# Local and strided attention with a gated MLP on one core: a constant tile of 636 bytes made 1024 bytes wide

## The chip, the core and the metric

The kernel runs on one core of a Trainium2 chip. A core has a matrix engine (TensorE, PE in the profile, with its weight loads listed apart as PEld), a vector engine (VectorE, DVE), a scalar engine (ScalarE, ACT), GpSimd (POOL) and SyncE (SP), which here issues the transfers. They share an on-chip memory of 128 partitions (SBUF) and the accumulators that TensorE writes (PSUM). The metric is the device time of one execution in microseconds, as the median of several runs. Addresses below are byte offsets inside a partition; they are the same in all 128 partitions.

## The reference

`q`, `k` and `v` have shape (8, 8, 576, 64): batch, heads, sequence, head dimension. The first four heads use a local mask of 32 positions, the other four a strided one; the result goes through a gated MLP whose gate is `erf(softplus(h))`.

```python
scores = scale * np.matmul(q, k.transpose(0, 1, 3, 2))
mask_local = (rel >= 0) & (rel < stride)                       # stride = 32
mask_strided = (rel >= 0) & (pos[None, :] % stride == pos[:, None] % stride)
masks = np.stack([mask_local if h < H // 2 else mask_strided for h in range(H)], axis=0)
scores = np.where(masks[None, :, :, :], scores, -1000000000.0)
scores = scores - np.max(scores, axis=-1, keepdims=True)
attn = np.exp(scores)
attn = attn / (np.sum(attn, axis=-1, keepdims=True) + 1e-09)
x = np.matmul(attn, v)                 # then (4608, 512)
h = x @ w_in                           # w_in 512 x 2048
sp = np.maximum(h, 0.0) + np.log1p(np.exp(-np.abs(h)))
out = (h * erf(sp)) @ w_out            # w_out 2048 x 512
```

## The kernel before

**The work.** The 4608 tokens are cut into 12 chunks of 384. For each chunk and each of 16 blocks of 128 hidden columns, `mm1` (L725) makes twelve matmuls: the weights are blocks of 128 columns of `pair` tiles (`w_in` split in a high and a low part), and the moving operand is a slice of 384 columns of `xhi` or `xlo`, the attention output in the same split. Four ACT tanh steps (L733) and DVE steps between them (L730, L754) form the gate; L757 and L760 split the product into `ghi` and `glo`. `mm2` (L788) then makes nine matmuls (three for each 128 tokens) with slices of `ghi` and `glo` as weights and 512 columns of a `pair` tile (`w_out`) as the moving operand. `mm1` runs 2304 matmuls in all, `mm2` 1728.

**Attention.** Batches 0 and 1 go through `piece`: scores (L302), the first mask added by TensorE (L312), a maximum over the partitions on POOL (L328), its subtraction (by TensorE with the tile `neg` for batch 0, by DVE for batch 1), exponential on ACT, product with `v` (L345). The other batches go through `quad`: scores (L502, in 64x64 tiles of the array, or L490), the second mask applied by a DVE minimum with the tile `cap` (L520), maximum and sum on POOL (L528, L548), product with `v` (L592). L617 and L622 write the result into `xhi` and `xlo`.

**The weights.** They arrive as 64-bit words in `words` tiles and are turned into 32-bit floats by DVE (L677, L684, L690), then split by ACT (L695) and DVE (L698) into `pair` tiles, which take the place of the `words` tiles in the same memory.

**What sets the order.** A planner (`Plan`) gives each operation an assumed duration and a key, works out one order for each engine and emits the instructions in it. Tiles' addresses do not enter it. SyncE issues all transfers from one queue in the planner's order.

**Where the tiles lie.** Pools give out addresses in the order in which tiles are first made, each rounded up to 32 bytes. In the built program the eight `xhi` and `xlo` tiles begin at 16512 and follow each other at 4608 bytes; `ident` is at 53376, `con` (first mask) at 53888, `cap` (second mask) at 54784. `cap` has 2·96 + 126 = 318 bf16 elements, 636 bytes, and so takes 640. Behind it stand `neg` at 55424, then two `qk` buffers (55936 and 58976), three `v` buffers (62016, 63072, 64128), the `sm`, `mx`, `tt` and `r` buffers of the attention, three `ob`, two `a`, two `ghi` and two `glo` buffers (79648 to 95007), and from 95008 on the 32 weight tiles `words`/`pair` of 4096 bytes each. The last one ends at 226080.

The lines that make the constants:

```python
con = cpool.tile([P, NCON], BF16, name="con")
cap = cpool.tile([P, 2 * QL + QS], BF16, name="cap")
cap_l = cap[:, : 2 * QL].rearrange("p (b h q) -> p b h q", b=2, h=1)
cap_s = cap[:, 2 * QL :].rearrange("p (u q) -> p u q", u=1)
neg = cpool.tile([P, P], F32, name="neg")
```

Of the kernel before, what the change touches and what calls it, by code (L numbers as in the profile page):

```python
# [10 lines left out]
BF16 = mybir.dt.bfloat16  # L11
# [7 lines left out]
P = 128  # L19
# [6 lines left out]
SW = 512  # L26
# [23 lines left out]
QL = 96  # L50
RB = 7
NA = S // 32
QS = RB * NA
# [143 lines left out]
def attention_moe(  # L197
# [13 lines left out]
    cpool = ctx.enter_context(tc.tile_pool(name="cpool", bufs=1))  # L211
# [11 lines left out]
    mask_l = con[:, : 2 * QL].rearrange("p (b h q) -> p b h q", b=2, h=1)  # L223
    mask_s = con[:, 2 * QL : 2 * QL + QS].rearrange("p (u q) -> p u q", u=1)
    ident_b = con[:, 2 * QL + QS :]
    cap = cpool.tile([P, 2 * QL + QS], BF16, name="cap")
    cap_l = cap[:, : 2 * QL].rearrange("p (b h q) -> p b h q", b=2, h=1)
    cap_s = cap[:, 2 * QL :].rearrange("p (u q) -> p u q", u=1)
    neg = cpool.tile([P, P], F32, name="neg")
# [792 lines left out]
```

## Time and profile before

| | us |
|---|---|
| median of 3 runs | 945.45 |
| the runs | 944.45 to 946.5 |
| the profiled execution's own time | 944.03 |
| its span, first to last instruction | 942.3 |
| TensorE busy in the span | 930.5 |
| DVE busy | 679.0 |
| ACT busy | 576.6 |
| POOL busy | 324.5 |

The span is what the profile covers; the profiled execution's own time is 1.73 us longer. "Busy" counts the time in which an engine had at least one instruction running, so an engine can be busy without working at its peak. The lists by line give a group's busy time, the mean duration of one instruction and the idle time ahead of it; the chain of waits follows the work back from the last instruction.

### The profile page before, as it was taken

The page shows a single profiled execution, that of the slowest core. Times are in us where ns is not written, and L with a number is a line of the kernel's source. Part 1 is how long each engine was busy: PE and PEld are TensorE (multiplying, and loading weights), DVE is VectorE, ACT ScalarE, POOL GpSimd, SP SyncE. Part 2 cuts the span into 40 slices and gives each one's busy share as a digit, 9 for nine tenths or more (in the row PEclk, how much of TensorE's full clock was granted, in tenths as well). Part 3 has the DMA queues.
Part 4 walks back from the last instruction along what each step waited for, and adds up shares of the span by engine and source line. Part 5 has one row for each costly group of instructions (what it writes and reads, how often), then busy time and mean ns, then how long its engine had stood idle before and what let it go on. Part 6 is the DMA issues. An engine that isn't in the chain of part 4 may idle for free.

```text
span 942.3 us, 16156 instructions
## 1 busy us (share of the span) xinstructions
PE 930.5 (99%) x5993; PEld 820.0 (87%) x5993; DVE 679.0 (72%) x1539; ACT 576.6 (61%) x1283; POOL 324.5 (34%) x160
## 2 busy tenths in 40 slices
PE   8999999999999999999999999999999999999998
PEld 6788898888888888888888888888888888999997
DVE  5999998667777777666867777775777776455553
ACT  4776677556566656556556655665655656555654
POOL 4443104525263444513535643342535353000000
PEclk9999999999999999999999999999999999999999
DMA  8987202111212113102112111211211210000000
GB/s 285 303 316 253 65 16 79 39 45 58 77 50 79 48 47 105 39 12 81 54 54 93 51 47 51 79 38 34 90 47 49 81 46 4 34 1 0 34 1 34
DMA packets 37663, 68.83 MB, mean 73 GB/s; under 512 B 4176, under 2 KB 18640, under 8 KB 37584
## 3 DMA queue, kind: packets, MB, share of 16 engines
q1 hardware_dynamic: 37584, 67.80, 22.0%
q8 instruction: 47, 0.77, 0.3%
q14 instruction: 32, 0.26, 0.1%
HBM read 58.34 MB, written 9.44 MB: 72 GB/s over the span
## 4 chain that ended last, share of the span: by engine, by line
PE 92%; DVE 5%; DMA 2%; ACT 0%; issue 0%; SPq 0%
PE o L788 42%; PE h L725 41%; PE ps L592 3%; PE ps L502 2%; DVE w L684 1%; DVE w L690 1%; PE s L302 1%; DVE w L677 1%; DVE a L730 1%; DVE pair L698 1%; DMA qk<-qk_str 1%; DMA words<-w_in 1%; PE ps L490 0%; DVE xlo L399 0%; PE ps L302 0%; PE av L345 0%
## 5 line engine op out<-in xcount | busy, mean ns | idle before, releaser
L788 PE MATMUL o<-pair,ghi 128*128 128x512 f32 x1152 | 366.3, 399 | 0.0
L733 ACT ACTIVATE a<-a 128x384 f32<-128x384 f32 x576 | 292.0, 522 | 94.4 <-DVE a L730 86.4
L730 DVE SCALAR_TENSOR_TENSOR a<-a,h 128x384 f32<-128x384 f32 x384 | 210.9, 550 | 170.7 <-ACT a L733 167.8
L725 PE MATMUL h<-xhi,pair 128*128 128x384 f32 x1536 | 303.7, 339 | 1.5 <-DVE glo L760 1.4
L725 PEld LDWEIGHTS h<-xhi,pair 128*128 128x128 f32 x1536 | 273.9, 188 | 10.5 <-DVE glo L760 2.3
L788 PEld LDWEIGHTS o<-pair,ghi 128*128 128x128 f32 x1152 | 209.5, 188 | 43.8 <-issue 1.5
L788 PE MATMUL o<-pair,glo 128*128 128x512 f32 x576 | 224.9, 390 | 0.0
L528 POOL PARTITION_ALL_REDUCE mx<-sm x66 | 100.0, 1558 | 357.3 <-DVE sm L520 348.4
L548 POOL PARTITION_ALL_REDUCE su<-sm x66 | 182.0, 2801 | 43.2 <-ACT sm L542 43.2
L733 ACT ACTIVATE a<-h 128x384 f32<-128x384 f32 x192 | 94.2, 491 | 148.7 <-PE h L725 148.2
L725 PE MATMUL h<-xlo,pair 128*128 128x384 f32 x768 | 166.3, 338 | 0.0
L725 PEld LDWEIGHTS h<-xlo,pair 128*128 128x128 f32 x768 | 138.1, 188 | 0.0
L754 DVE TENSOR_TENSOR h<-a,h 128x384 f32<-128x384 f32 x192 | 106.9, 557 | 42.2 <-ACT a L733 42.1
L788 PEld LDWEIGHTS o<-pair,glo 128*128 128x128 f32 x576 | 108.2, 188 | 24.2
L757 ACT CAST ghi<-h 128x384 fp32r<-128x384 f32 x192 | 91.3, 476 | 59.0 <-PE o L788 57.7
L760 DVE TENSOR_TENSOR glo<-h,ghi 128x384 fp32r<-128x384 f32 x192 | 105.4, 549 | 20.2 <-ACT ghi L757 16.7
L328 POOL PARTITION_ALL_REDUCE mx<-sm x24 | 42.4, 1776 | 63.0 <-ACT sm L320 55.5
L542 ACT ACTIVATE sm<-sm 128x384 f32<-128x384 f32 (+2 forms) x66 | 36.2, 553 | 18.6 <-DVE sm L535 17.8
L535 DVE TENSOR_TENSOR sm<-sm,mx 128x384 f32<-128x384 f32 (+2 forms) x66 | 39.9, 614 | 0.2
L520 DVE TENSOR_TENSOR sm<-ps,cap 128x384 f32<-128x384 f32 (+2 forms) x66 | 37.0, 586 | 0.0
L592 PEld LDWEIGHTS ps<-sm,v 128*64 128x64 f32 x528 | 24.6, 136 | 9.2 <-issue 6.7
L592 PE MATMUL ps<-sm,v 128*64 128x96 f32 (+2 forms) x528 | 31.7, 260 | 0.0
(59 smaller groups left out, 532.6 us busy)
## 6 DMA issues: line engine op xcount, KB each, us to landing
qk<-qk_loc SPq DMA_DIRECT2D x48, 304.0 KB, 3.2
qk<-qk_str SPq DMA_DIRECT2D x32, 380.0 KB, 3.7
v<-v_all SPq DMA_DIRECT2D x80, 130.0 KB, 2.2
out<-ob SPq DMA_DIRECT2D x36, 256.0 KB, 2.1
words<-w_in SPq DMA_DIRECT2D x16, 512.0 KB, 5.1
words<-w_out SPq DMA_DIRECT2D x16, 512.0 KB, 4.6
qk<-qk_str SPq DMA_DIRECT2D x16, 136.0 KB, 2.6
v<-v_all SPq DMA_DIRECT2D x16, 65.0 KB, 1.9
```

What stands on the lines that cost most here:

```text
L328: yield nc.gpsimd.partition_all_reduce(mx[:, :cols], sm[:, :cols], P, ReduceOp.max)
L528: yield nc.gpsimd.partition_all_reduce(mx[k][:, :cols], sm[k][:, :cols], P, ReduceOp.max)
L535: yield nc.vector.tensor_tensor(out=d, in0=d, in1=mx[k][:, :cols], op=ALU.subtract)
L548: yield nc.gpsimd.partition_all_reduce(su[k][:, :cols], sm[k][:, :cols], P, ReduceOp.add)
L592: yield nc.tensor.matmul(px[h * D : (h + 1) * D, c0 : c0 + n], v[i][:, blk, h, :D], sm[bank][:, c : c + n], start=True, stop=True,)
L725: yield nc.tensor.matmul(ph[:, :CH], win[4 * s + cc][:, w, fs], x[cc][:, c0 : c0 + CH], start=(i == 0), stop=(i == len(terms) - 1))
L730: yield nc.vector.scalar_tensor_tensor(out=out, in0=in0, scalar=scalar, in1=in1, op0=op0, op1=op1)
L733: yield nc.scalar.activation(dst, src, func, bias=bias[i], scale=scale)
L754: yield nc.vector.tensor_tensor(out=ph[:, :CH], in0=a.tile, in1=ph[:, :CH], op=ALU.mult)
L757: yield nc.scalar.copy(ghi.tile, ph[:, :CH])
L760: yield nc.vector.tensor_tensor(out=glo.tile, in0=ph[:, :CH], in1=ghi.tile.bitcast(F32), op=ALU.subtract)
L788: yield nc.tensor.matmul(po.tile, g[:, ts], wout[f][:, w], start=(f == 0 and i == 0), stop=(f == NFC - 1 and i == 2),)
```

## The change

`cap` is made with 512 bf16 columns (1024 bytes) instead of 318, and the name `cap` then stands for its first 318 columns. Everything that writes or reads `cap` sees the same 318 columns at the same address, 54784. Every tile behind it begins 384 bytes higher: `neg` at 55808 instead of 55424, the first weight tile at 95392 instead of 95008, and so on to the last, which ends at 226464. `xhi`, `xlo`, `ident`, `con` and `cap` stay where they were. The built programs hold the same instructions in the same order, with the same waits, on all five engines.

384 is three times 128, so every moved address keeps its remainder by 128 and changes it by 256 and by 512. The weight tiles go from 288 to 160 in remainders by 512.

```diff
-    cap = cpool.tile([P, 2 * QL + QS], BF16, name="cap")
+    cap = cpool.tile([P, SW], BF16, name="cap")[:, : 2 * QL + QS]
```

`SW` is 512, `QL` 96 and `QS` 126.

## The prediction, on record before the change was run

> **What bounds the kernel now.** I read the page's totals first.
>
> ```profile
> span 942.3 us, 16156 instructions
> ...
> PE 930.5 (99%) x5993; PEld 820.0 (87%) x5993; DVE 679.0 (72%) x1539; ACT 576.6 (61%) x1283; POOL 324.5 (34%) x160
> ...
> PEclk9999999999999999999999999999999999999999
> ...
> PE 92%; DVE 5%; DMA 2%; ACT 0%; issue 0%; SPq 0%
> ```
>
> TensorE has something running in 99% of the span, its granted clock is full in every slice, and 92% of the chain that ended last is TensorE's. The remaining 7% are DVE and transfers. The view of busy time by stretches (PE, PEld, DVE, ACT, POOL) tells where they lie:
>
> ```profile
> 0.00:33.00 33.00, 27.84 (x176) 20.78 (x177) 22.19 (x52) 18.61 (x52) 15.68 (x13) 1.00 0.87 280
> 33.00:74.00 41.00, 38.78 (x260) 33.14 (x258) 40.63 (x96) 30.54 (x82) 15.55 (x8) 1.00 0.92 327
> 74.00:116.00 42.00, 41.38 (x275) 35.63 (x274) 41.84 (x103) 26.57 (x62) 11.39 (x7) 1.00 0.44 140
> 116.00:790.00 674.00, 674.00 (x4549) 596.39 (x4549) 499.02 (x1147) 413.39 (x904) 281.83 (x132) 1.00 0.18 56
> 790.00:942.30 152.30, 148.53 (x742) 134.08 (x738) 75.31 (x146) 87.48 (x185) 0.00 (x0) 1.00 0.04 16
> ```
>
> Two stages have different limits. From 116 to 790 us TensorE is busy in all 674.00 us, and nearly so to the end; DVE, ACT, POOL and the transfers (busy shares of 0.18 and 0.04) only have to keep up. Up to 116 us the transfers are at 0.87 and 0.92 of their time at first, and then DVE is: 40.63 of 41 us and 41.84 of 42 us. There DVE unpacks the weights, and its durations set the end. So a change of addresses matters if it alters the pace of TensorE's 4032 large matmuls, DVE's instructions before 116 us, or a transfer of the first 33 us. It cannot matter through a slightly slower ACT or POOL later on.
>
> **The change part by part.** It adds no instruction, no transfer, no byte moved and no wait, and the order on each engine is the same; only addresses differ. Four effects have to be costed.
>
> *The instructions that use `cap` itself.* `cap` does not move, and its 318 columns stay next to each other.
>
> ```profile
> L829 DVE TENSOR_SCALAR cap<-con_f x1: 321/321/321, 3.9 to 3.9; 128x318 bf16<-128x318 f32 x1
> L830 DVE TENSOR_TENSOR cap<-cap,con_f x1: 492/492/492, 4.3 to 4.3; 128x318 bf16<-128x318 bf16 x1
> ```
>
> These handle 318 columns and will still do so (the added 194 columns are never touched): 0 us. The 66 masks that read `cap` later do the same work at the same place: 0 us.
>
> *The pace of the large matmuls.* The chain in order of time shows them in runs (start, length, group):
>
> ```profile
> 105.65 2.11 PE h L725 x12
> ...
> 118.20 4.33 PE h L725 x24
> ...
> 123.22 2.12 PE h L725 x12
> ...
> 145.48 4.24 PE h L725 x24
> ...
> 150.53 4.35 PE o L788 x18
> ...
> 159.74 4.31 PE o L788 x18
> ...
> 919.85 4.24 PE h L725 x24
> ```
>
> A run of 24 `mm1` matmuls takes 4.24 us, or 176.7 ns each, at 145 us and at 920 us alike: next to 282 us of POOL work and transfers as without either. Between those runs the weights come from other `pair` tiles and `x` from another third of `xhi`. So neither the neighbours' traffic nor, at the distances that occur (multiples of 512 bytes), the address shows in the pace. What the large matmuls do not show is an address with another remainder by 256 or 512, since all their weights begin at 288 by 512, the moving operand of `mm1` at 128 and that of `mm2` at 288. After the change those that moved begin at 160. The nearest rows with mixed remainders are the weight loads of the attention:
>
> ```profile
> L502 PEld LDWEIGHTS ps<-qk x960: 129/135/135, 115.2 to 771.7; 64*64 64x64 f32 x192
> ...
> L592 PEld LDWEIGHTS ps<-sm,v x528: 132/137/139, 149.6 to 789.8; 128*64 128x64 f32 x176
> ...
> L725 PEld LDWEIGHTS h<-xhi,pair x1536: 186/188/192, 43.6 to 929.1; 128*128 128x128 f32 x192
> ```
>
> The columns are minimum, median and maximum in ns. L502 reads its weights from ten remainders by 512 (0, 64, 96, 128, 224, 256 and others), L592 from twelve; the slowest load is 6 or 7 ns above the fastest, and the maximum is within 2 ns of the median. For L725, which has one remainder, the spread is 6 ns too. So a spread of this size needs no address to explain it. I take 0 for the pace. The bounds come from the runs above: the shortest is 2.11 us for 12 against 2.12, which is 0.8 ns each and over 2304 matmuls 1.9 us less; the longest is 4.33 for 24 against 4.24, which is 3.75 ns each and over 2304 matmuls 8.6 us more. `mm2`'s 4.31 and 4.35 for 18 are 2.2 ns each, 3.8 us over 1728. I take zero because 0.8 and 3.75 ns occur here with the address remainders unchanged.
>
> *DVE's instructions before 116 us.* The four steps that unpack weights, first by mean and then by minimum, median and maximum:
>
> ```profile
> L684 DVE SCALAR_TENSOR_TENSOR w<-words,w 128x512 uint32<-128x512 uint32 x32 | 23.7, 741 | 0.1
> L690 DVE SCALAR_TENSOR_TENSOR w<-words,w 128x512 uint32<-128x512 uint32 x32 | 23.0, 718 | 0.1
> L698 DVE TENSOR_TENSOR pair<-w,pair 128x512 fp32r<-128x512 f32 x32 | 22.1, 692 | 0.5 <-ACT pair L695 0.2
> ...
> L677 DVE TENSOR_SCALAR w<-words 128x512 uint32<-128x512 uint32 x32 | 16.4, 514 | 7.1 <-DMA words<-w_in 7.1
> ```
>
> ```profile
> L684 DVE SCALAR_TENSOR_TENSOR w<-words,w x32: 653/684/1316, 8.6 to 137.7; 128x512 uint32<-128x512 uint32 x32
> ...
> L690 DVE SCALAR_TENSOR_TENSOR w<-words,w x32: 655/682/1195, 9.4 to 139.2; 128x512 uint32<-128x512 uint32 x32
> ...
> L677 DVE TENSOR_SCALAR w<-words x32: 390/424/1216, 8.2 to 136.3; 128x512 uint32<-128x512 uint32 x32
> ...
> L698 DVE TENSOR_TENSOR pair<-w,pair x32: 653/680/882, 13.5 to 140.8; 128x512 fp32r<-128x512 f32 x32
> ```
>
> The means lie above the medians by 741−684 = 57, 718−682 = 36, 692−680 = 12 and 514−424 = 90 ns, together 195 ns; 32 times that is 6.2 us. This excess sits in a few long instances, and they coincide with POOL's reductions:
>
> ```profile
> 55.25 1.97 POOL L328 PARTITION_ALL_REDUCE mx<-sm  x1 [3.44 <-ACT sm L320]
> 55.34 2.16 DVE L677 TENSOR_SCALAR w<-words 128x512 uint32<-128x512 uint32 x2
> ```
>
> Two L677 take 2.16 us where two medians are 0.85, and end just behind POOL's 57.22 us. What decides here is which instruction starts inside a reduction, not where its tile lies. As the order is unchanged, I take 0; if no instance or twice as many met a reduction, the ends would be −6.2 and +6.2 us. Since DVE has no idle time there, this would reach the end nearly in full.
>
> *The transfers of the first stage.* Two are on the chain:
>
> ```profile
> 17.85 6.23 DMA qk<-qk_str
> ...
> 28.97 4.99 DMA words<-w_in
> ```
>
> They carry the same bytes in the same queue order, so 0 us. The ends I take from the start of DVE's saturation: all of the 7.1 us that L677 waited for `words` gained, or as much lost. [...]
>
> [...]
>
> **The sum.** 0 + 0 + 0 + 0 = 0. Against the profiled execution's own time: 942.3 of span + 1.73 around it = 944.03, unchanged. That execution is 1.42 us below the median of the runs, 945.45, so on the median's scale the forecast is **945.4 us**.
>
> **The rivals.** *Faster: the start falls out differently.* A transfer that lands some 0.1 us earlier shifts which DVE step meets a POOL reduction. For it speaks that DVE is full from 33 to 116 us, and that 6.2 us of excess are there to be had; against it that the order is kept and that as many could be added as removed. If half the excess went, 3.1 us: 942.3 us. Chance 0.11.
>
> *Slower: weights and `x` get in each other's way.* In `mm1` the weights (in `pair`) move by 384 bytes while the operand that streams (`xhi`, `xlo`) stays, so their distance changes for the first time to one that is no multiple of 512 from those tried. If TensorE read both through something that is cut by address, each of the 2304 matmuls could pay; at the 3.75 ns of the longest run that is 8.6 us: 954.0 us. For it speaks that nothing in this trace has tried the new distance; against it L502 and L592, whose many remainders do not show, and the unchanging 4.24 us. It decides from 0.8 ns for each matmul (1.9 us in all): a run of 24 would then take 4.26 us or more. Chance 0.09, in which I also put the start falling out worse.
>
> *No change* has 0.80: no price above is other than zero without a mechanism that the trace does not show.
>
> **How the numbers follow.** What a measurement of this kernel can tell from no change is about 0.2%, 1.9 us, so "within" means 943.6 to 947.3. Faster 0.11, same 0.80, slower 0.09. The range leaves the far ends (−6.2, +8.6) to the rivals' 0.2 in all and holds the likeliest case with the spread of the three runs (944.45 to 946.5) and about a microsecond of change in the start on either side: **943.0 to 948.0 us**.
>
> **What would show it.** Right: 24 `mm1` in 4.24 us and 18 `mm2` in 4.31 to 4.35, PE busy near 930.5, DVE's four unpacking steps with the same medians, and a first matmul run without gaps near 116 us. The pace rival shows as 4.26 or more for 24 (or 4.22 and less, if it helps), evenly from 145 to 930 us. The start's rival shows as other means with the same medians for L677, L684 and L690, and as everything behind 116 us shifted by one amount. A change of DVE's or ACT's medians without a change of the end would say that addresses matter to those engines but not to this kernel. The prediction is wrong if the median leaves 943.6 to 947.3.

## The result

| | us |
|---|---|
| before, median of 4 runs | 944.95 (943.53 to 946.5) |
| changed, median of 4 runs | 936.74 (934.98 to 937.15) |
| ratio | 0.9909, 95% interval 0.9888 to 0.993 |

The changed kernel is faster by 0.9%, some 8 us. The prediction was no change, 943.0 to 948.0 us. One later run of the kernel before, slow at 3900.2 us, is left out below.

The profile after, the page's totals:

```profile
span 933.2 us, 16156 instructions
...
PE 921.7 (99%) x5993; PEld 813.2 (87%) x5993; DVE 678.5 (73%) x1539; ACT 576.7 (62%) x1283; POOL 323.3 (35%) x160
...
PEclk9999999999999999999999999999999999999999
...
PE 92%; DVE 6%; DMA 1%; ACT 0%; issue 0%; SPq 0%
```

The span is 9.1 us shorter, TensorE's busy time 8.8 us; DVE (679.0 to 678.5), ACT (576.6 to 576.7) and POOL hardly move. The granted clock is full in both (1.000). Busy time by stretches after:

```profile
33.00:74.00 41.00, 38.73 (x256) 32.87 (x255) 40.74 (x94) 30.74 (x84) 15.66 (x8) 1.00 0.93 323
74.00:116.00 42.00, 41.38 (x274) 35.58 (x273) 41.85 (x103) 26.70 (x62) 11.42 (x7) 1.00 0.44 140
116.00:790.00 674.00, 674.00 (x4581) 596.70 (x4581) 502.30 (x1159) 417.27 (x913) 281.62 (x132) 1.00 0.18 56
```

The limits are those of before: DVE from 33 to 116 us (busy in 40.74 of 41 and 41.85 of 42 us), TensorE behind it (674.00 of 674 us). But from 116 to 790 us TensorE gets through 4581 matmuls instead of 4549 while it is as fully busy. The chain of waits shows how (start, length, group; three of the chain's largest pieces, then one from its first 150 us):

```profile
144.38 4.17 PE h L725 x24
...
158.47 4.33 PE o L788 x18
...
176.89 4.30 PE o L788 x18
```

```profile
122.37 2.08 PE h L725 x12
```

24 `mm1` matmuls take 4.17 or 4.18 us instead of 4.24, from 144 us to the end. 18 `mm2` take 4.30 to 4.33 instead of 4.31 to 4.35; 30 shorter runs of 18 take 4.08 to 4.13 instead of 4.11 to 4.13.

To divide the gain exactly, I took the times from each matmul's start to the next one's start from both traces. From the 241st `mm1` (at 147.4 us before, 146.3 after) to the last matmul they add up as follows:

| from the 241st mm1 on | before, us | after, us | difference |
|---|---|---|---|
| starting at an `mm1` matmul (2064) | 369.69 | 363.60 | −6.09 |
| starting at an `mm2` matmul (1583) | 370.41 | 368.58 | −1.83 |
| starting at an attention matmul (1480) | 50.59 | 50.60 | 0.00 |

7.9 of the 9.1 us lie there, three quarters of them in `mm1`. The other 1.1 us were gained before the 241st `mm1`, 0.7 of them already at the first one (43.6 us before, 42.9 after).

What did not change is as telling. The weight loads of `mm1` after:

```profile
L725 PEld LDWEIGHTS h<-xhi,pair x1536: 186/188/192, 42.8 to 920.1; 128*128 128x128 f32 x192
```

The load has the same minimum, median and maximum as before, though the matmuls follow each other 3 ns faster (173.67 instead of 176.69 ns). The medians of DVE's unpacking steps are within 10 ns of those before:

```profile
L684 DVE SCALAR_TENSOR_TENSOR w<-words,w x32: 653/678/1315, 8.6 to 136.9; 128x512 uint32<-128x512 uint32 x32
...
L677 DVE TENSOR_SCALAR w<-words x32: 390/414/1219, 8.1 to 135.5; 128x512 uint32<-128x512 uint32 x32
```

### The profile page after: what moved, and what is told of

The parts are those of the page before. It is cut to its first block, busy times and chain, and to the rows that moved or that the text cites. A ratio compares the mean times of both kernels' runs of the same rounds, so it can differ in the third digit from the quotient of the medians.

```text
span 933.2 us, 16156 instructions
## 1 busy us (share of the span) xinstructions
PE 921.7 (99%) x5993; PEld 813.2 (87%) x5993; DVE 678.5 (73%) x1539; ACT 576.7 (62%) x1283; POOL 323.3 (35%) x160
## 4 chain that ended last, share of the span: by engine, by line
PE 92%; DVE 6%; DMA 1%; ACT 0%; issue 0%; SPq 0%
PE o L788 43%; PE h L725 41%; PE ps L592 3%; PE ps L502 2%; DVE w L684 1%; DVE w L690 1%; PE s L302 1%; DVE w L677 1%; DVE a L730 1%; DVE pair L698 1%; DMA qk<-qk_str 1%; DMA words<-w_in 1%; PE ps L490 0%; PE warm L916 0%; DVE xlo L399 0%; PE ps L302 0%
## 5 line engine op out<-in xcount | busy, mean ns | idle before, releaser
L725 PE MATMUL h<-xhi,pair 128*128 128x384 f32 x1536 | 299.5, 337 | 1.5 <-DVE glo L760 1.4
L725 PEld LDWEIGHTS h<-xhi,pair 128*128 128x128 f32 x1536 | 270.0, 188 | 10.7 <-DVE glo L760 2.7
L725 PE MATMUL h<-xlo,pair 128*128 128x384 f32 x768 | 164.5, 336 | 0.0
L725 PEld LDWEIGHTS h<-xlo,pair 128*128 128x128 f32 x768 | 135.9, 188 | 0.0
L592 PEld LDWEIGHTS ps<-sm,v 128*64 128x64 f32 x528 | 24.6, 136 | 9.3 <-issue 6.5
L592 PE MATMUL ps<-sm,v 128*64 128x96 f32 (+2 forms) x528 | 31.7, 260 | 0.0
```

Source lines behind the costliest of these rows:

```text
L592: yield nc.tensor.matmul(px[h * D : (h + 1) * D, c0 : c0 + n], v[i][:, blk, h, :D], sm[bank][:, c : c + n], start=True, stop=True,)
L725: yield nc.tensor.matmul(ph[:, :CH], win[4 * s + cc][:, w, fs], x[cc][:, c0 : c0 + CH], start=(i == 0), stop=(i == len(terms) - 1))
```

## The experiments

Below, *distance* is the address of a matmul's weights minus that of its moving operand, by 256 bytes. Before, it is 288 − 128 = 160 in `mm1` and 288 − 288 = 0 in `mm2`; in the change 160 − 128 = 32 and 0. *Pace* is the mean time from the start of one matmul to the start of the next of the same line, from the trace; times over 250 ns, in which something else is waited for, are left out (14 of 2196 for `mm1`, 83 of 1602 for `mm2`). Before it is 176.69 and 229.26 ns, after 173.67 and 228.02. Where both distances were run again at other addresses the pace came back within 0.05 ns, while single executions scatter by more (the kernel before took 943.06 to 947.04 us), and most kernels below ran once. So the pace carries the verdicts.

**Which addresses count?** Three theories: the distance (A), the weights' own address (B), or the place of DVE's and ACT's tiles (C). Four kernels tell them apart; the kernel before took 944.85 us beside them.

*All tiles moved by 384 bytes, `xhi` and `xlo` too:*

```diff
+    cpool.tile([P, 192], BF16, name="padx")
     xhi = [cpool.tile([P, RING], F32R, name=f"xhi{c}") for c in range(NCC)]
```

> A pad of 384 bytes ahead of xhi, cap as before: every tile moves by 384, xhi and xlo too. Weights of mm1 at 160 by 512 (as in the change), moving operand at 0, distance 160 (as before). Theory A (what counts is the distance between the weights and the moving operand of a matmul): as before, 24 mm1 in 4.24 us, about 945 us. Theory B (what counts is the remainder of the weights' own address): as the change, 4.17 us for 24, about 937 us. Theory C (what counts is where the tiles of DVE and ACT stand to xhi and xlo): about 945 us.

942.68 us, pace 176.68 and 229.30: that of before, although the weights stand at 160 by 512 as in the change. The time is 2.2 us below that of the kernel before; its 145th `mm1` began 1.4 us earlier (116.6 instead of 118.0 us).

```profile
237.03 4.24 PE h L725 x24
...
260.22 4.35 PE o L788 x18
```

*Only the weight tiles moved by 384 bytes:*

```diff
+    wpool.tile([P, 192], BF16, name="padw")
     bias = (T1B, T2B, T3B, T4B)
```

> A pad of 384 bytes ahead of the first weight tile alone: only the 32 weight tiles move; neg, the buffers of the attention, ob, a, ghi and glo stay. Theories A and B: mm1 as in the change, 24 in 4.17 us. Theory C: 4.24 us and 945 us. In mm2 the distance between its weights (ghi, glo) and its moving operand (pair) is now 128 off; if A holds for mm2 as for mm1, its 18 leave 4.31 to 4.35 us, and the end is anywhere from 930 to 945 us.

943.91 us, pace 174.00 and 232.48. `mm1` gains nearly as in the change, with DVE's and ACT's tiles, the weight tiles apart, where they were, so C falls. `mm2`, whose distance is now 128 instead of 0, loses 3.2 ns for each of 1728 matmuls, 5.6 us, and that eats most of the gain: `mm2` depends on its operands' distance too.

```profile
238.16 4.18 PE h L725 x24
...
247.13 4.17 PE h L725 x24
251.93 4.39 PE o L788 x18
```

*`xhi` and `xlo` moved by 128, everything behind `cap` by 512:*

```diff
+    cpool.tile([P, 64], BF16, name="padx")
     xhi = [cpool.tile([P, RING], F32R, name=f"xhi{c}") for c in range(NCC)]
...
-    cap = cpool.tile([P, 2 * QL + QS], BF16, name="cap")
+    cap = cpool.tile([P, 512], BF16, name="cap")[:, : 2 * QL + QS]
```

> 128 bytes ahead of xhi and cap made 384 bytes wider: xhi and xlo move by 128 (remainder 256 by 512), everything behind cap by 512, so the weights keep the remainder 288 of before, and the distance becomes 32, that of the change. Theory A: as the change, 4.17 us for 24, about 937 us. Theory B: as before, 4.24 us, about 945 us. Theory C: as the change.

937.43 us, pace 173.65 and 228.02, that of the change, although the weights have the remainder 288 of before. With the first kernel this settles it against B.

```profile
238.91 4.17 PE h L725 x24
...
252.57 4.33 PE o L788 x18
```

*`cap` widened to 768 bytes, so a move by 128:*

```diff
-    cap = cpool.tile([P, 2 * QL + QS], BF16, name="cap")
+    cap = cpool.tile([P, 384], BF16, name="cap")[:, : 2 * QL + QS]
```

> cap made 768 bytes wide: all tiles behind it move by 128 instead of 384. Weights of mm1 at 416 by 512, distance 288 by 512 and 32 by 256. If the effect (by distance or by own remainder) repeats every 256 bytes: as the change, 4.17 us for 24, about 937 us. If it repeats every 512 bytes only: nothing is forced; 4.24 us if 160 and 288 are alike.

936.0 us, pace 173.63 and 228.03, the change again: 128 and 384 differ by 256, and that makes no difference here (173.63 and 173.67 ns).

*`cap` widened to 896 bytes, a move by 256*, is the counterpart: it moves the same tiles and keeps both distances.

```diff
-    cap = cpool.tile([P, 2 * QL + QS], BF16, name="cap")
+    cap = cpool.tile([P, 448], BF16, name="cap")[:, : 2 * QL + QS]
```

> cap made 896 bytes wide: all tiles behind it move by 256, so that both distances by 256 stay as before (160 and 0) while every address behind cap, and its remainder by 512, is new. If the distance by 256 is all that counts: 24 mm1 in 4.24 us, 18 mm2 in 4.31 to 4.35 us, about 945 us. If a wider cap helps as such, or remainders by 512 count: 4.17 us and about 937 us.

945.09 us (before beside it: 945.86), pace 176.68 and 229.25: both as before.

```profile
239.45 4.24 PE h L725 x24
...
262.63 4.35 PE o L788 x18
```

The kernel before, the change and the four of these that keep `mm2` at distance 0 fall into two paces, and the distance by 256 in `mm1` alone sorts them: 176.68 to 176.69 ns at 160, 173.63 to 173.67 at 32.

**How does the price follow the distance?** The pad ahead of the weight tiles was given the other multiples of 32, which moves both distances at once.

```diff
+    wpool.tile([P, PAD // 2], BF16, name="padw")      # PAD = 32, 64, 96, 160, 192, 224
     bias = (T1B, T2B, T3B, T4B)
```

> Only the weight tiles move, by 32 bytes, so that the distances by 256 (weights minus moving operand) are 192 in mm1 and 224 in mm2. So far mm1 takes 176.7 ns at 160 and 173.7 at 32; mm2 takes 228.0 to 229.3 at 0 and 232.5 at 128. If there are two halves (below 128 fast, from 128 on slow, one and the same for both): mm1 near 176.7, mm2 near 232.5, about 950 us. If the price grows step by step with the distance, mm1 lies above 173.7 and differs from 176.7 by 1 ns or more. If a step of 32 bytes counts for nothing, all is as before: 945 us.

> Weight tiles moved by 96: distances 0 in mm1 and 160 in mm2. Two halves: mm1 173.7, mm2 near 232.5, about 943 us. Step by step: mm1 another value than at 32.

> Weight tiles moved by 160: distances 64 in mm1 and 96 in mm2. Two halves: mm1 173.7, mm2 228 to 229, about 937 us. Step by step: mm1 between its values at 32 and 160, mm2 between those at 0 and 128.

> Weight tiles moved by 224: distances 128 in mm1 and 32 in mm2. Two halves: mm1 176.7, mm2 228 to 229, about 945 us. Step by step: mm1 another value than at 160.

> Weight tiles alone moved by 192: distances 96 in mm1 and 64 in mm2, two values not seen yet. If every mm2 distance other than 0 is dear: mm2 at 232 to 234 ns on the mean, and with an mm1 of 174 to 176 ns 943 to 949 us. If mm2 rises gradually from 0 (32 and 96 are 233.0 and 233.9): also 233 to 234.

> Weight tiles alone moved by 64: distances 224 in mm1 and 192 in mm2, the two values not seen yet. If mm2 is cheap at 0 alone: 232 to 234 ns on the mean for it, 18 in 4.38 us or more where a chain of 24 follows. If mm1 is dear only around 128 to 160: 173.4 to 174.3 ns for it; 942 to 946 us in all.

The kernel before took 944.85 to 945.86 us beside these.

| weights moved by | mm1 distance | mm1 pace, ns | mm2 distance | mm2 pace, ns | one execution, us |
|---|---|---|---|---|---|
| 0 (before) | 160 | 176.69 | 0 | 229.26 | 944.9 |
| 32 | 192 | 173.38 | 224 | 233.12 | 941.2 |
| 64 | 224 | 175.12 | 192 | 229.39 | 941.1 |
| 96 | 0 | 174.25 | 160 | 233.48 | 945.89 |
| 160 | 64 | 174.07 | 96 | 233.85 | 946.31 |
| 192 | 96 | 173.83 | 64 | 233.39 | 945.17 |
| 224 | 128 | 176.17 | 32 | 233.03 | 949.36 |
| 384 | 32 | 174.00 | 128 | 232.48 | 943.91 |

The two halves that I had offered are refuted: 192 is `mm1`'s cheapest distance and 32 one of `mm2`'s dear ones. So is "`mm2` is cheap at 0 alone": 192 is as good. `mm1` is dear at 128 and 160, cheap elsewhere, and at 224 in between (175.12 ns, where 173.4 to 174.3 was expected); `mm2` is cheap at 0 and 192 and dear elsewhere, by 3 to 4 ns. The two lines do not follow one curve. The paces do explain the times: for the worst kernel, 2304 · (176.17 − 176.69) + 1728 · (233.03 − 229.26) ns = +5.3 us over the 944.86 of before, 950.2; 949.36 was measured. The same sum comes within 0.9 us for all but one: moved by 32 it gives 943.9, and 941.2 was measured, with a 145th `mm1` that began 1.9 us earlier than before. The worst kernel's chain:

```profile
239.11 4.23 PE h L725 x24
...
252.98 4.39 PE o L788 x18
```

**What does a line take from the other line?** The table cannot explain one thing: `mm2`'s distance is 0 before and after, and yet its pace falls from 229.26 to 228.02 ns. The traces show where, in the runs of 24 and 18 from the 241st `mm1` on. The last eight times from start to start in a run of 18 `mm2` are 227.0 ns on the mean before and 226.9 after. The second to ninth fall from 230.6 to 226.7 in the 24 runs that stand directly behind `mm1`, and only from 231.1 to 230.4 in the 50 behind attention matmuls. So once a run is under way `mm2` goes as its own distance has it, and what it gained it gained at the start of its runs, behind `mm1` above all. For `mm1`, whose runs of 24 all stand behind `mm2`, it is alike: the 12th to 23rd time is 176.67 ns in all three kernels with all of `mm1` at distance 160 and 173.33 in all four at 32, while the first eleven at 32 are 173.8 ns on the mean where `mm2` is at 0 and 174.7 where it is at 128. Why a run's first matmuls go at another pace is not shown.

**Do the two prices add up?** A cheap distance for each, by the smallest step of the original edit.

```diff
-    cap = cpool.tile([P, 2 * QL + QS], BF16, name="cap")
+    cap = cpool.tile([P, 336], BF16, name="cap")[:, : 2 * QL + QS]
```

> cap widened to 672 bytes, all tiles behind it move by 32: distances 192 in mm1 and 0 in mm2, each the cheapest value seen so far (173.4 ns in the run with the weights moved by 32, and 228.0 in the change). If the two prices are set by the two distances alone and simply add: 24 mm1 in 4.16 to 4.17 us, 18 mm2 in 4.30 to 4.33 us, 936 to 937 us, level with the change. If the change owes its gain to more than the distances: above 938 us.

936.37 us (median of 4 runs), ratio 0.9906 (0.988 to 0.9932) to before, pace 173.39 and 228.35. A move by 32 bytes does what the move by 384 does. The two are level; neither is shown to beat the other.

```profile
237.43 4.16 PE h L725 x24
...
251.11 4.31 PE o L788 x18
```

**Is it a matter of single matmuls?** `mm1` runs through the moving tiles 0 to 3, and its slowness before is uneven. Two kernels gave only one of the four a better distance: the moving tile 1, or the weights that go with moving tile 2. The tiles after each kept their remainders by 256.

```diff
-    xhi = [cpool.tile([P, RING], F32R, name=f"xhi{c}") for c in range(NCC)]
+    xhi = [cpool.tile([P, RING + 64 * (c == 1)], F32R, name=f"xhi{c}")[:, 32 * (c == 1) :][:, :RING] for c in range(NCC)]
```

(and the same for `xlo`)

> As before, but xhi1 and xlo1 alone begin 128 bytes higher (the tiles around them are spaced so that every other tile keeps its remainder by 256). Before, the time from a matmul's start to the next one's start is by moving tile 174 (number 0), 180 (1), 175 (2) and 178 ns (3). If the distance between a matmul's own moving operand and the weights counts, matmul by matmul: number 1 falls from 180 to 173 or 174, the others stay; 24 mm1 in 4.20 us, about 941.5 us. If the whole stream has to be at a good distance: no change, 4.24 us.

```diff
-            return pools[pool].tile(shape, dtype, tag=tag, name=name, bufs=bufs[tag])
+            return (as before) if tag not in ("w2", "w6", "w10", "w14") else pools[pool].tile([P, 2 * SW + 64], dtype, tag=tag, name=name, bufs=bufs[tag])[:, 32 : 2 * SW + 32].rearrange("p (a b) -> p a b", a=shape[1])
```

> As before, but the weight tiles of w_in that go with xhi2 and xlo2 alone begin 128 bytes higher. The weights of matmul 2 are loaded while matmul 1 streams. If a load meets the stream that runs during it: the time from matmul 1's start to 2's falls from 180 to 173 or 174 ns, and that from 2 to 3 stays at 175. If a matmul is slow because of its own weights' address: 1 stays at 180 and 2 changes. 24 mm1 in about 4.20 us in the first case, 941.5 us.

Mean time from start to next start in the second half of the runs of 24 (the 12th to 23rd time), by the moving tile of the first of the two:

| ns | 0 | 1 | 2 | 3 | mean of these | pace of all |
|---|---|---|---|---|---|---|
| before | 174.3 | 179.9 | 175.0 | 177.4 | 176.67 | 176.69 |
| moving tile 1 by 128 | 177.5 | 176.4 | 177.5 | 175.0 | 176.58 | 176.18 |
| weights of 2 by 128 | 175.0 | 175.9 | 180.0 | 175.8 | 176.67 | 176.50 |
| the change (all) | 173.3 | 173.3 | 173.3 | 173.3 | 173.33 | 173.67 |

They took 941.98 and 943.12 us beside 945.15; the paces account for 2.3 and 0.9 us of that (−0.5 and −0.2 ns on `mm1`, −0.6 and −0.3 on `mm2`), the rest is within the scatter of single executions. The time that I aimed at, from 1 to 2, fell in both, from 180 to 176 ns, but not to 173 or 174, and that from 2 to 3 grew, from 175 to 177.5 and 180. Of the 4.20 us for 24 that I expected, 4.23 or 4.24 was measured. Once a run was under way, what one matmul saved was lost again at its neighbours: the mean is 176.6 or 176.7 ns as before. The small gain lies in the first half of the runs and behind them.

In `mm1` the traces before and after record nearly every weight load from 2 to 4 ns behind the start of the matmul before it, and it takes 186 to 192 ns while that matmul takes some 338, so the weights of 2 load while 1 runs. In both kernels that load has the distance 32 to moving tile 1, and every other load keeps 160 to the tile of the matmul that it runs beside. If this pair of reads alone counted, the two kernels would show one pattern. They show two, so the single-tile kernels do not tell which reads meet.

## Why the prediction was wrong

**What bounds the kernel** was right: TensorE from 116 us on (busy in 674.00 of 674 us up to 790, after), DVE from 33 us to there (82.59 of 83 us). Of the 9.1 us that the span lost, 7.9 lie in the pace of the large matmuls from the 241st `mm1` on.

**The instructions of `cap`**: right, 0 us.

**The pace: here the prediction failed.** "I take 0 for the pace" should have been −3.0 ns for `mm1` and −1.2 ns for `mm2`; over the matmuls from the 241st `mm1` on that was 6.1 and 1.8 us. The step that led there was reading the steady 4.24 us as proof that the address has no effect. The loss was there all the time, of the same size in every run, since all weights and all moving operands of `mm1` had one distance by 256, in all tiles and all thirds of `xhi`. A row that never varies the quantity cannot bound its effect. The lower bound of 0.8 ns, drawn from such rows, was a quarter of what came. For `mm2`, whose distance stayed at 0, the sum had no term either; what came there came in the first matmuls of its runs.

The other support was unfit too. The durations of weight loads, which were read in L502 and L592, do not show the effect: L725's own loads are 186/188/192 ns before and after. It shows between the starts of matmuls, and in part in the matmuls' own durations (median 338 ns before, 336 after in `mm1`).

**The start** was costed at 0 with "about a microsecond" of scatter. 0.7 us came at the first `mm1`. In the fourteen other kernels' traces the 145th `mm1` starts anywhere from 116.1 to 119.7 us (118.0 before, 117.2 after) without relation to the distances, so I count it as scatter. L677's wait for `words` is 7.1 us before and 5.0 after; in those kernels it lies between 4.9 and 8.7. DVE's medians, as forecast, hardly moved. The reading of the excess was right, and better than the one instance showed: before, 17 unpacking steps last over 60 ns longer than their line's median, 6.4 us in all, and every one of them overlaps a POOL reduction. After, it is again 17 steps and 6.4 us, each on a reduction.

**The rivals.** The slower rival had the right quantity and the wrong sign: the distance between weights and moving operand of `mm1` goes with its pace, but the dear distance was the one before (176.69 ns at 160), and the change left it (173.67 ns at 32). The list of signs did name the other direction ("4.22 and less, if it helps"), and 4.17 came; but it had no chance of its own, although "their distance changes" holds either way. The faster rival (the start) is not what happened.

**The transfers** were taken at 0, with 7.1 us gained or lost as the ends. A packet that carries a strided `qk` row (3040 bytes) takes 120 ns in the trace at the lower quartile, median and upper quartile, before and after.

**What stays open.** Why the distance counts is not shown. That it does, and that a move by 256 bytes leaves the pace of `mm1` as it was (176.68 and 176.69 ns), would fit a weight load and the stream beside it getting in each other's way; that is a guess of mine, no run saw it, and the two single-tile kernels do not fit the simplest form of it. Why `mm1` and `mm2` have different cheap distances is not shown; their streams have different lengths (384 and 512 columns). In the single-tile kernels a delay avoided at one matmul (180 to 176 ns) turned up at the next one (175 to 177.5 and 180 ns); whether the position of a load within the stream matters, no run tried. Why a run's first matmuls go at another pace than its later ones is open too. Steps finer than 32 bytes were not tried.

## What to carry over

In this kernel, where TensorE is busy in 99% of the span, the addresses of weights and moving operands are a tuning parameter: a pad of 32, 128 or 384 bytes behind the moving operand of `mm1` was worth 0.9%, and a pad of 224 bytes ahead of the weight tiles alone cost 0.5% (one run, borne out by the paces). Look at the time from one matmul's start to the next, not at the durations of the loads (186/188/192 ns before and after), and scan pads in 32-byte steps over 256 bytes, with the pad between the two operands and not ahead of both (384 bytes ahead of both left `mm1` at 176.68 ns). And when a row of the profile is taken as proof that an address does not count, see first whether that row ever varied the address in the way the change does.

## What was not expected of the hardware

In these runs the pace of back-to-back fp32r matmuls with 128 columns of weights depends on the distance between the two operands by 256 bytes: 173.4 to 176.7 ns with 384 moving columns, 228.0 to 233.9 ns with 512. Where both lines have equal distances, it repeats within 0.05 ns at different addresses; where only its own is equal, a line's pace still varies by 0.4 (`mm1` at 32) to 1.3 ns (`mm2` at 0), through the first matmuls of its runs. In the two single-tile kernels a delay avoided at one matmul was paid by the next ones once a run was under way (180 to 176 ns at one, 175 to 177.5 or 180 at its neighbour).
